# Opening of a spectral-filter-plus-MLP kernel: transposes paired by part, part of the first transform done early, another order for the weights

## The chip, the cores and the metric

The kernel runs on one core of a Trainium2 chip. A core has five engines with an instruction queue each: TensorE (PE in the profile, its weight loads PEld), VectorE (DVE), ScalarE (ACT), GpSimd (POOL) and SyncE (SP), which here only issues DMAs. The time is device microseconds (us) of one launch. Three runs of the kernel before took 394.82, 395.14 and 395.75 us; the median, 395.14 us, is the time that the prediction is set against.

## The reference, cut to what matters

```python
def reference(A_x, A_w_r, A_w_i, B_x, B_w1, B_b1, B_w2):
    x = A_x                                   # 1 x 2048 x 512, float32
    xn = (x - mean) / sqrt(var + 1e-5)        # over the last axis
    X = rfft2(xn) * (A_w_r + 1j * A_w_i)      # spectral filter over both axes
    h = einsum("bsd,df->bsf", xn, B_w1) + B_b1        # 512 -> 1792
    act = h * tanh(softplus(h))                       # Mish
    return x + irfft2(X, s=(2048, 512)) + einsum("bsf,fd->bsd", act, B_w2)
```

Every matrix product is made from float16 parts: a float32 operand is split into a high part and a low part (what the high part leaves over), and three products (high by high, high by low, low by high) are summed in PSUM. To fit float16's range a weight matrix is scaled by a power of two that is taken from a norm of it.

## The kernel before, in words

**Tiling.** The 2048 rows are four groups g of four row tiles of 128. The MLP is worked as 56 up tiles (g, f): hidden chunk f (14 chunks of 128) for the 512 rows of group g, twelve matmuls of 512 columns (three products for each of four blocks dc of the input, `mlp_up`, L744), and 56 down tiles (`mlp_down`, L800) that add a chunk's part of the output into four PSUM banks `pa`, twelve matmuls again. For group 0 and even f the down tile takes its four matmuls with the low part of w2 last (L806). A call b(1) runs one up or one down tile, whichever `mlp_all` (L837) picks: the first E_UP = 11 are up tiles, then ups and downs by a lag and by free buffers for the activations `a`. An up tile's sum `ph` lives in a pool of two PSUM banks (`ps_h`, L53), which the transposes of row tiles (`pt`) also use. `activate` (L761) follows an up tile: Mish on ACT (`hb`, L767), the high part of `a` on ACT (L785), its low part on DVE (L788).

**Opening** (`first_group`, L226). Rows of group 0 are normalised: the high part of a row tile on ACT (L239), its float32 value on DVE (`normed`, L249) and from that the low part on DVE (`low`, L254). PE transposes each part in four 128-column pieces (`turn_`). One PSUM bank `pt[s]` holds the high and low part of one row tile s; DVE copies the high half out and ACT the low half (`copy`, L261) into `xnT`, the moving operand of the up tiles. Matmuls on a tile of zeros (`idle_matmuls`, L221) fill PE between them. Meanwhile ACT squares w1's chunks 0 and 1 for their norm (L396), POOL sums over partitions (L326), DVE makes the scale (`w1_scale`, L411) and ACT and DVE split chunk 0 into high (`split_hi`) and low (`split_lo`). w1 comes in seven chunks of 256 hidden columns, c = f // 2; chunks 2 to 6 have a norm of their own (`w1_norm(1)`): two by squares on ACT, three by BN_STATS on DVE (L403). `act_scale` (L432) bounds the hidden values from these norms, for the scale of `a`. All of w2 must have a norm (`norm_w2`, L447) before its first split.

**The order** on ACT and DVE (in the opening also on PE) is the order in which the code is written (`in_order`, L67), so an instruction that waits holds all behind it on its engine.

**Slots** (L1023). After the opening, 26 slots of one b(1) each carry the rest of the preparation: statistics of the next group (`sums`, `factors`), normalising (`norm`, L202, with the low part on POOL), transposes (`turned_rows`, L297, copied out by DVE at L306), the first transform step of every row tile (`s1_forward`, L137, three matmuls into `psS`, from a pool of two banks `ps_f`; evicted by ACT and DVE at L123, L127, L128 in `butterfly`) and w2's chunks (high part on ACT, L468; low part on DVE one slot later, L471). In a slot come first the tile, then the last slot's leftovers (copies of `pt`, low parts of `a`, evictions of `psS`, low part of w2), then this slot's own work. The row tiles of group 0 have their transform step in slots 0 to 3.

**After the slots**, `stream_a` (L911) runs the middle transform steps with MLP tiles between them, and the end runs the last inverse step (`s1_inverse`) with the last tiles.

Of the kernel before, what the change touches and what calls it, by code (L numbers as in the profile page):

```python
# [41 lines left out]
def spectral_mlp_kernel(ctx, tc, x, wt, w0, w1, b1, w2, cT, cIT, cM, out):  # L42
# [183 lines left out]
    def first_group(ts):  # L226

        pe, act, dve = mybir.EngineType.PE, mybir.EngineType.Activation, mybir.EngineType.DVE
        with in_order(pe, act, dve):
            idle_matmuls(29)  # L230
            mv, rs, nb = factors(0, sums(0, ts, range(4)))
            xh, xs, pt = {}, {}, {}
            xnT[0] = cp.tile([P, 2, 4, 512], F16, tag="xnT0", name="xnT_0")
            xTv = xnT[0].rearrange("p h c (s t) -> p h c s t", s=4)

            def high(s):

# [14 lines left out]

            def low(s):
                nc.vector.tensor_sub(xh[s][:, 1, :], xs[s], xh[s][:, 0, :])  # L254

            def turn_(s, h):
                if not h:
                    pt[s] = ps_h.tile([P, 2, 4, P], F16, tag="h", name=f"pt_{s}")
                turn(pt[s], xh[s], h)

            def copy(s):  # L261
                nc.vector.tensor_copy(xTv[:, 0, :, s, :], pt[s][:, 0])
                return nc.scalar.copy(xTv[:, 1, :, s, :], pt[s][:, 1])


            qs = w1_norm(0, lambda: high(0))
            for s in range(1, 4):
                high(s)
            normed(0)
            normed(1)  # L270
            low(0)
            turn_(0, 0)
            turn_(1, 0)
            turn_(0, 1)
            low(1)
            turn_(1, 1)
            idle_matmuls(6)
            copy(0)
            w1_scale(0, qs)
            normed(2)  # L280
            normed(3)
            split_hi(0)
            low(2)
            turn_(2, 0)
            idle_matmuls(4)
            turn_(2, 1)
            copy(1)
            low(3)
            turn_(3, 0)
            idle_matmuls(2)  # L290
            turn_(3, 1)
            idle_matmuls(2)
            copy(2)
            ends = [copy(3).ins, split_lo(0).ins]
        return [xh[s] for s in range(4)], ends

    def turned_rows(g, s, xh):  # L297
        if s == 0:
# [88 lines left out]
    def w1_norm(k, between=None):  # L387

        a, b = W1_PARTS[k]
        n = min(b - a, 3)  # L390
        q = sp.tile([P, n], F32, tag=f"qw{k}", name=f"qw1_{k}")
        for c in range(a, a + 2):
            if between and c > a:
                between()
            fs = slice(2 * c * P, (2 * c + 2) * P)
            nc.scalar.activation(w1t[:, 0, :, fs], w1st[c], AF.Square, accum_out=q[:, c - a : c - a + 1])  # L396
        if b - a > 2:
            m = b - a - 2
            st = sp.tile([P, 2 * m, 6], F32, tag="stw", name="stw")
            for c in range(a + 2, b):  # L400
                v = w1st[c].rearrange("p c f -> p (c f)")
                for h in range(2):
                    nc.vector.bn_stats(st[:, 2 * (c - a) - 4 + h, :], v[:, 512 * h : 512 * h + 512])  # L403
            mv = sp.tile([P, 2], F32, tag="mvw", name="mvw")
            nc.vector.bn_aggr(mv, st)
            t = q[:, 2:3]
            nc.vector.scalar_tensor_tensor(t, mv[:, 0:1], mv[:, 0:1], mv[:, 1:2], op0=ALU.mult, op1=ALU.add)
            nc.vector.tensor_scalar(t, t, 1024.0 * m, None, op0=ALU.mult)
        return sum_of(f"w1_{k}", q, n)

    def w1_scale(k, t):  # L411
        p1 = pow2_norm(f"w1_{k}", t, min(W1_PARTS[k][1] - W1_PARTS[k][0], 3))
# [19 lines left out]
    def act_scale():  # L432
# [4 lines left out]
        nc.vector.scalar_tensor_tensor(hb_, pmx, 46.0, sc["mba"], op0=ALU.mult, op1=ALU.add)  # L437
        pH = pow2_of("H", hb_)
        sc["a"] = over("a", pH, 14)
        sc["pH"] = pH  # L440
# [297 lines left out]


    macc, yacc, last, wait, in_a = {}, {}, {}, [], []  # L740
    sc["ahead"], sc["staged"] = True, False
    staged, lows = [], []

    def mlp_up(g, f, acts):  # L744
# [1 line left out]
        ph = ps_h.tile([P, 512], F32, tag="h", name=f"ph_{g}_{f}")  # L746

        steps = [(dc, p) for dc in range(4) for p in range(3)]
        if g == f == 0:
            steps = [(dc, p) for p in range(3) for dc in range(4)]  # L750
        for n, (dc, p) in enumerate(steps):
            hs, hm = ((0, 0), (0, 1), (1, 0))[p]
# [8 lines left out]
    def activate(g, f, acts, ph, last_mm):  # L761
# [16 lines left out]
        wait.append((a, hb))  # L778
        if g == 0 and f < 2:
            return  # L780
        if g == 0 and f in (2, 3):
            split_w1(f)
        while wait:
            a, hb = wait.pop(0)
            hi = nc.scalar.activation(a[:, 0, :], hb, AF.Copy, scale=sc["a"])  # L785
# [51 lines left out]
    def mlp_all():  # L837
# [4 lines left out]
        while down < len(tiles):  # L842
# [4 lines left out]
            if free and up < len(tiles) and (up < E_UP or up - down < lag or (n_down >= 2 and up - down > lag)):  # L847
# [95 lines left out]
    load_w1(1)  # L943
    nc.sync.dma_start(cMt[:, O_ID:], cM[:, O_ID:])
    nc.sync.dma_start(b1t, b1)
    for c in range(2, 7):
        load_w1(c)
    load_ct(0)
    for c in range(7):
        load_w2(c)  # L950
    xs = {1: load_x(1)}
    xhs, ends = first_group(xs0)
    with tc.issue_after(ends[0]), tc.issue_after(ends[1]), in_order(mybir.EngineType.Activation, mybir.EngineType.DVE):

# [43 lines left out]
    for g, (a, ns, ts) in {  # L998
# [19 lines left out]
    copies, evict, low_w2 = [], [], []  # L1018
# [242 lines left out]
```

## Time and profile before

| quantity | value |
|---|---|
| median of three runs | 395.14 us (394.82 to 395.75) |
| the profiled execution | 394.64 us, of which its span (first to last instruction) 392.9 us |
| PE busy | 379.6 us, 97% of the span |
| DVE, ACT, POOL busy | 248.3, 203.8, 59.8 us (63%, 52%, 15%) |
| DMA | 61.61 MB, mean 157 GB/s |
| granted TensorE clock, mean over the span | 0.998 of full speed |

Times in the views are us from the span's start. A row of the timeline merges like instructions that follow each other on an engine: start, length, engine, line, operation, output and inputs, shapes, count, and in brackets the engine's idle time before it with what ended that. Matmuls are pipelined: a row of n matmuls is as long as n steps from start to start plus the rest of the last one, which is longer than a step. So time lost by PE is read from starts, not from the bracket alone.

### The profile page before, as it was taken

Reading aid. Unit: us, or ns where it says so; the run is one execution under the profiler, and the core shown is the slowest. Engines: PE = TensorE matmul, PEld = TensorE weight load, DVE = VectorE, ACT = ScalarE, POOL = GpSimd, SP = SyncE. Lnnn points to the kernel's source line nnn. Section 1 sums busy time; section 2 is a strip of 40 time slices with the busy share of each in tenths; the row PEclk is TensorE's granted clock in tenths of the full one; section 3 lists DMA queues with packets and bytes.
Section 4 is the critical chain, followed back from the end, with each engine's and each line's share of the span. In section 5 each row is a group of like instructions: output and inputs, shape, how many; then the busy total and the mean of one; then the engine's idle time right before and its main releaser. Section 6 shows DMA issues by size and latency. Waiting matters only on the chain. (4 is left out here: it accounts for less than half of the span.)

```text
span 392.9 us, 6538 instructions
## 1 busy us (share of the span) xinstructions
PE 379.6 (97%) x2481; PEld 190.7 (49%) x2481; DVE 248.3 (63%) x532; ACT 203.8 (52%) x325; POOL 59.8 (15%) x61
## 2 busy tenths in 40 slices
PE   8799999999999999999999999999999999999995
PEld 3344444545545454456444565455554546434442
DVE  5789793868578426974797535965449863324334
ACT  3869849677544336563554636365464455422110
POOL 0000015644523300000111100121001110210000
PEclk9999999999999999999999999999999999999999
DMA  8996021555347982066722727227561023654556
GB/s 280 364 395 276 1 82 45 171 178 163 103 133 231 249 236 81 24 147 159 237 82 62 201 64 211 83 81 197 180 188 55 27 82 91 205 160 138 165 194 253
DMA packets 49519, 61.61 MB, mean 157 GB/s; under 512 B 3776, under 2 KB 36032, under 8 KB 48848
## 3 DMA queue, kind: packets, MB, share of 16 engines
q1 hardware_dynamic: 49488, 61.20, 50.5%
q8 instruction: 19, 0.31, 0.3%
q14 instruction: 12, 0.10, 0.1%
HBM read 44.38 MB, written 16.78 MB: 156 GB/s over the span
## 5 line engine op out<-in xcount | busy, mean ns | idle before, releaser
L753 PE MATMUL ph<-xnT,w1t 128*128 128x512 f16 x672 | 153.5, 379 | 1.0 <-DVE w1t L352 0.5
L753 PEld LDWEIGHTS <-w1t 128*128 128x128 f16 x672 | 64.7, 98 | 78.2 <-DVE w1t L352 1.0
L88 PE MATMUL pa<-w2r,a 128*128 128x512 f16 x196 | 74.4, 380 | 0.0
L91 PE MATMUL pa<-w2r,a 128*128 128x512 f16 x196 | 74.4, 379 | 0.0
L92 PE MATMUL pa<-w2r,a 128*128 128x512 f16 x196 | 74.3, 379 | 0.0
L788 DVE SCALAR_TENSOR_TENSOR a<-hb,sc_a,a 128x512 f16<-128x512 f32 x56 | 42.2, 757 | 50.1 <-ACT a L785 49.8
L767 ACT ACTIVATE hb<-ph,b1t,sc_exp 128x512 f32<-128x512 f32 x56 | 43.2, 771 | 57.6 <-PE ph L753 57.5
L133 POOL TENSOR_TENSOR tt<-bt_t,tt 128x512 f16<-128x512 f32 x16 | 19.8, 1240 | 184.2 <-ACT tt L132 177.9
L785 ACT ACTIVATE a<-hb,sc_a 128x512 f16<-128x512 f32 x56 | 40.1, 720 | 1.5
L92 PEld LDWEIGHTS <-a 128*128 128x128 f16 x196 | 19.2, 98 | 22.5
L88 PEld LDWEIGHTS <-a 128*128 128x128 f16 x196 | 19.1, 98 | 21.9 <-issue 0.8
L91 PEld LDWEIGHTS <-a 128*128 128x128 f16 x196 | 19.2, 98 | 21.2 <-issue 0.8
L351 ACT ACTIVATE u<-r,sc_u 128x512 f16<-128x512 f32 x16 | 11.5, 720 | 23.9 <-DVE r L651 16.4
L133 POOL TENSOR_TENSOR y<-bt_s,y 128x512 f16<-128x512 f32 x16 | 19.1, 1194 | 31.4 <-ACT y L132 28.7
L132 ACT CAST y<-bt_s 128x512 f16<-128x512 f32 x16 | 9.9, 617 | 21.1 <-DVE bt_s L128 17.3
L808 PE MATMUL pa<-w2r,a 128*128 128x512 f16 x84 | 19.4, 379 | 0.6 <-DVE w2r L471 0.3
L132 ACT CAST tt<-bt_t 128x512 f16<-128x512 f32 x16 | 9.9, 616 | 15.9 <-DVE bt_t L128 13.5
L887 DVE SCALAR_TENSOR_TENSOR m<-psY,sc_k,m 128x512 f32<-128x512 f32 x12 | 8.7, 747 | 14.9 <-PE psY L92 14.9
L210 POOL TENSOR_TENSOR xh<-xs,xh 128x512 f16<-128x512 f32 x12 | 15.6, 1305 | 15.8 <-ACT xh L209 14.4
L706 DVE SCALAR_TENSOR_TENSOR at<-psA,at 128x512 f16<-128x512 f32 x16 | 10.7, 688 | 8.8 <-ACT at L705 8.8
L583 ACT ACTIVATE ix<-psD 64x512 f32<-64x512 f32 x16 | 9.5, 594 | 10.9 <-PE psD L571 10.7
L705 ACT ACTIVATE at<-psA 128x512 f16<-128x512 f32 x16 | 9.1, 590 | 10.5 <-issue 5.9
(146 smaller groups left out, 519.5 us busy)
## 6 DMA issues: line engine op xcount, KB each, us to landing
wt<-in_wt_dram SPq DMA_DIRECT2D x32, 256.0 KB
x<-in_x_dram SPq DMA_DIRECT2D x8, 512.0 KB
d_y<-y SPq DMA_DIRECT2D x16, 256.0 KB
wm<-in_wt_dram SPq DMA_DIRECT2D x8, 512.0 KB
yt<-d_y SPq DMA_DIRECT2D x16, 256.0 KB
d_a<-at SPq DMA_DIRECT2D x32, 128.0 KB
ai<-d_a SPq DMA_DIRECT2D x16, 256.0 KB
d_t<-tt SPq DMA_DIRECT2D x16, 256.0 KB
```

The source lines that it names most:

```text
L88: first = nc.tensor.matmul(ps, stat(0), mov(0), start=start, stop=False)
L91: nc.tensor.matmul(ps, stat(0), mov(1), start=False, stop=False)
L92: return nc.tensor.matmul(ps, stat(1), mov(0), start=False, stop=stop)
L132: nc.scalar.copy(out[:, :, 0, :], tv)
L133: nc.gpsimd.tensor_sub(out[:, :, 1, :], tv, out[:, :, 0, :])
L210: nc.gpsimd.tensor_sub(xh[:, 1, :], xs, xh[:, 0, :])
L351: hi = nc.scalar.activation(dst_h, src, AF.Copy, scale=scale)
L753: last_mm = nc.tensor.matmul(ph, w1t[:, hs, dc, f * P : (f + 1) * P], xnT[g][:, hm, dc, :], start=n == 0, stop=n == 11)
L767: nc.scalar.activation(hb, ph, AF.Mish, bias=b1t[:, f : f + 1], scale=s_exp[k])
L785: hi = nc.scalar.activation(a[:, 0, :], hb, AF.Copy, scale=sc["a"])
L788: lo = nc.vector.scalar_tensor_tensor(a[:, 1, :], hb, sc["a"], a[:, 0, :], op0=ALU.mult, op1=ALU.subtract)
L808: nc.tensor.matmul(pacc[g][s], a[:, ha, rows[s]], w2t[:, f // 2, hw, 0, :], start=f == n == 0, stop=False)
```

## The change

- The two row tiles 2k and 2k+1 share PSUM banks by part: `pt[k, 0]` holds both high parts, `pt[k, 1]` both low parts. One DVE copy (`copy_hi`) and one ACT copy (`copy_lo`) of 1024 columns stand for two each of 512.
- High parts of row tiles 0 and 1 are both made on ACT ahead of the square of w1's chunk 1. The order of the other steps changes, and 8 idle matmuls stand where 14 stood.
- The first transform step of row tiles 2 and 3 runs in the opening, beside their last transposes; its evictions run in slot 0. Its constants (`load_ct(0)`) are loaded ahead of w1's chunks 2 to 6 instead of after them. Row tiles 0 and 1 follow in slots 1 and 2.
- For three chunks of w1 the norm takes maxima (TENSOR_REDUCE) instead of BN_STATS, and `act_scale` has 92 for 46.
- Twelve up tiles come first instead of eleven. Splits of w1 and norms of w2 stand in another order among them; the splits of chunk 1 and 3 no longer hang on `activate`.
- For group 0 every even up tile takes its products part by part (four matmuls of each), so the low part of its w1 chunk is needed at the ninth matmul instead of the third; before, tile 0 alone did.
- No up tile of a group starts before the copies of that group's four row tiles are in the program (`sc["rows"]`); with this, tile 14 (group 1, chunk 0) comes later among the down tiles.

```diff
-E_UP = 11
+E_UP = 12
@@ first_group
             def turn_(s, h):
-                if not h:
-                    pt[s] = ps_h.tile([P, 2, 4, P], F16, tag="h", name=f"pt_{s}")
-                turn(pt[s], xh[s], h)
-
-            def copy(s):
-                nc.vector.tensor_copy(xTv[:, 0, :, s, :], pt[s][:, 0])
-                return nc.scalar.copy(xTv[:, 1, :, s, :], pt[s][:, 1])
+                if s % 2 == 0:
+                    pt[s // 2, h] = ps_h.tile([P, 4, 2, P], F16, tag="h", name=f"pt_{s}_{h}")
+                for dc in range(4):
+                    nc.tensor.transpose(pt[s // 2, h][:, dc, s % 2, :], xh[s][:, h, dc * P : (dc + 1) * P], ident)
+
+            def copy_hi(k):
+                nc.vector.tensor_copy(xTv[:, 0, :, 2 * k : 2 * k + 2, :], pt[k, 0])
+
+            def copy_lo(k):
+                return nc.scalar.copy(xTv[:, 1, :, 2 * k : 2 * k + 2, :], pt[k, 1])

-            qs = w1_norm(0, lambda: high(0))
-            for s in range(1, 4):
-                high(s)
+            qs = w1_norm(0, lambda: (high(0), high(1)))
+            high(2)
+            high(3)
             normed(0)
             normed(1)
             low(0)
+            low(1)
             turn_(0, 0)
             turn_(1, 0)
             turn_(0, 1)
-            low(1)
             turn_(1, 1)
-            idle_matmuls(6)
-            copy(0)
-            w1_scale(0, qs)
+            idle_matmuls(3)
+            copy_hi(0)
             normed(2)
             normed(3)
-            split_hi(0)
+            copy_lo(0)
             low(2)
             turn_(2, 0)
+            idle_matmuls(1)
+            turn_(3, 0)
+            w1_scale(0, qs)
+            split_hi(0)
             idle_matmuls(4)
+            low(3)
+            copy_hi(1)
             turn_(2, 1)
-            copy(1)
-            low(3)
-            turn_(3, 0)
-            idle_matmuls(2)
+            evict = [s1_forward(0, 2, xh[2])]
             turn_(3, 1)
-            idle_matmuls(2)
-            copy(2)
-            ends = [copy(3).ins, split_lo(0).ins]
+            evict.append(s1_forward(0, 3, xh[3]))
+            ends = [copy_lo(1).ins, split_lo(0).ins]
@@ w1_norm
-            for c in range(a + 2, b):
-                v = w1st[c].rearrange("p c f -> p (c f)")
-                for h in range(2):
-                    nc.vector.bn_stats(st[:, 2 * (c - a) - 4 + h, :], v[:, 512 * h : 512 * h + 512])
-            nc.vector.bn_aggr(mv, st)
...
+        for c in range(a + 2, b):
+            nc.vector.tensor_reduce(q[:, c - a : c - a + 1], w1st[c], axis=AX.XY, op=ALU.max, apply_absolute_value=True)
         if b - a > 2:
+            nc.vector.tensor_mul(q[:, 2:n], q[:, 2:n], q[:, 2:n])
@@ mlp_up, activate, mlp_all
-        if g == f == 0:
+        if g == 0 and f % 2 == 0:
             steps = [(dc, p) for p in range(3) for dc in range(4)]
...
-        if g == 0 and f in (2, 3):
-            split_w1(f)
...
+            free = free and up < len(tiles) and tiles[up][0] <= sc["rows"]
@@ the loads and the opening's tiles
+    load_ct(0)
     for c in range(2, 7):
         load_w1(c)
-    load_ct(0)
...
         bias_max()
+        qs = w1_norm(1)
         split_w1(1)
-        w1_scale(1, w1_norm(1))
+        b(2)
+        w1_scale(1, qs)
+        split_hi(2)
         act_scale()
-        b(4)
+        split_lo(2)
+        b(2)
+        split_w1(3)
         norm_w2(3)
+        b(1)
         norm_w2(4)
         b(1)
         split_w1(4)
+        norm_w2(0)
+        b(1)
         norm_w2(5)
+        norm_w2(1)
         b(1)
-        norm_w2(0)
+        split_w1(5)
         norm_w2(6)
         b(1)
-        split_w1(5)
-        b(1)
-        norm_w2(1)
         norm_w2(2)
         b(1)
@@ the slots
-    for s in range(4):
-        at[s]["turn"].append((0, s))
+    for s in range(2):
+        at[s + 1]["turn"].append((0, s))
```

What stands on ACT in the opening before, from the first copy of a low part (`pt`, into `xnT`) on; `w1s_k` is w1's chunk k, L420 and L351 are high parts, L396 squares, `hb_0_f` the Mish of up tile f:

```order
L263 COPY xnT_0_187<-pt_0_206 128x4x128
L420 ACTIVATE w1t_92<-w1s_0_100,sc_w1_0_240 128x4x256
L263 COPY xnT_0_187<-pt_1_211 128x4x128
L263 COPY xnT_0_187<-pt_2_250 128x4x128
L263 COPY xnT_0_187<-pt_3_267 128x4x128
L351 ACTIVATE w1t_92<-w1s_1_102,sc_w1_0_240 128x4x256
L396 ACTIVATE w1t_92,qw1_1_293<-w1s_2_106 128x4x256 x2
L767 ACTIVATE hb_0_0_342<-ph_0_0_329,b1t_94,sc_exp_0_242 128x512
L767 ACTIVATE hb_0_1_358<-ph_0_1_345,b1t_94,sc_exp_0_242 128x512
L767 ACTIVATE hb_0_2_374<-ph_0_2_361,b1t_94,sc_exp_0_242 128x512
L351 ACTIVATE w1t_92<-w1s_2_106,sc_w1_1_315 128x4x256
```

And the same place on ACT now:

```order
L267 COPY xnT_0_187<-pt_0_1_216 128x4x256
L420 ACTIVATE w1t_92<-w1s_0_100,sc_w1_0_253 128x4x256
L267 COPY xnT_0_187<-pt_2_1_265 128x4x256
L403 ACTIVATE w1t_92,qw1_1_288<-w1s_2_107 128x4x256 x2
L358 ACTIVATE w1t_92<-w1s_1_102,sc_w1_0_253 128x4x256
L768 ACTIVATE hb_0_0_312<-ph_0_0_299,b1t_94,sc_exp_0_255 128x512
L768 ACTIVATE hb_0_1_328<-ph_0_1_315,b1t_94,sc_exp_0_255 128x512
L420 ACTIVATE w1t_92<-w1s_2_107,sc_w1_1_337 128x4x256
L768 ACTIVATE hb_0_2_366<-ph_0_2_353,b1t_94,sc_exp_0_255 128x512
```

Four copies became two of twice the size, and the high part of chunk 2 moved ahead of the Mish of tile 2.

On DVE in slots 4 to 7 before stand the evictions of the first transform step (`bt_s1_s`, row tile s), the low parts of w2 (L471, here chunks 2 and 3), the copy of row tile 4's transpose (L306) and the low part of up tile 12's `a`:

```order
L127 SCALAR_TENSOR_TENSOR bt_s1_2_685<-psS1_2_662,bc_s1_2_683 128x4x64
L128 SCALAR_TENSOR_TENSOR bt_s1_2_685<-psS1_2_662,bc_s1_2_683 128x4x64
L471 SCALAR_TENSOR_TENSOR w2r_93<-w2r_93,sc_w2_515 128x1024
L127 SCALAR_TENSOR_TENSOR bt_s1_3_716<-psS1_3_697,bc_s1_3_714 128x4x64
L128 SCALAR_TENSOR_TENSOR bt_s1_3_716<-psS1_3_697,bc_s1_3_714 128x4x64
L471 SCALAR_TENSOR_TENSOR w2r_93<-w2r_93,sc_w2_515 128x1024
L306 COPY xnT_1_764<-pt_4_765 128x8x128
L788 SCALAR_TENSOR_TENSOR a_0_12_780<-hb_0_12_778,sc_a_327,a_0_12_780 128x512
L127 SCALAR_TENSOR_TENSOR bt_s1_4_799<-psS1_4_774,bc_s1_4_797 128x4x64
```

And on DVE now, around the same two low parts of w2:

```order
L787 SCALAR_TENSOR_TENSOR a_0_12_680<-hb_0_12_678,sc_a_350,a_0_12_680 128x512
L127 SCALAR_TENSOR_TENSOR bt_s1_1_698<-psS1_1_674,bc_s1_1_696 128x4x64
L128 SCALAR_TENSOR_TENSOR bt_s1_1_698<-psS1_1_674,bc_s1_1_696 128x4x64
L471 SCALAR_TENSOR_TENSOR w2r_93<-w2r_93,sc_w2_522 128x1024
L787 SCALAR_TENSOR_TENSOR a_0_13_750<-hb_0_13_748,sc_a_350,a_0_13_750 128x512
L471 SCALAR_TENSOR_TENSOR w2r_93<-w2r_93,sc_w2_522 128x1024
L311 COPY xnT_1_771<-pt_4_772 128x8x128
L127 SCALAR_TENSOR_TENSOR bt_s1_4_801<-psS1_4_781,bc_s1_4_799 128x4x64
```

The low part of up tile 13 now stands ahead of w2's chunk 3 and of the first copy of group 1; before it stood far behind both. On PE the tiles in slots 0 to 12 were down 0, 1, up 11, down 2, 3, 4, up 12, down 5, up 13, down 6, 7, 8, up 14; they are now down 0, 1, up 12, down 2, 3, up 13, down 4, 5, 6, 7, 8, up 14, down 9.

## Rows read from the trace of the kernel before

**Rows 1.** The page: span, busy time of the engines, GB/s in 40 slices.

```profile
span 392.9 us, 6538 instructions
...
PE 379.6 (97%) x2481; PEld 190.7 (49%) x2481; DVE 248.3 (63%) x532; ACT 203.8 (52%) x325; POOL 59.8 (15%) x61
...
GB/s 280 364 395 276 1 82 45 171 178 163 103 133 231 249 236 81 24 147 159 237 82 62 201 64 211 83 81 197 180 188 55 27 82 91 205 160 138 165 194 253
```

**Rows 2.** Waits of PE: line, waited for, us in total, times, longest.

```profile
PE psT L88 <- DMA ai<-d_a: 1.8, 3, 0.9
```

**Rows 3.** Timeline of PE, opening and slots.

```profile
1.17 8.46 PE L224 MATMUL ps_warm<-warm 128*128 128x512 f16 x29 [1.17 <-DVE warm L219]
...
11.73 1.12 PE L215 MATMUL pt<-cMt,xh 128*128 128x128 f16 x12 [1.34 <-ACT xh L239]
...
17.77 10.96 PE L753 MATMUL ph<-xnT,w1t 128*128 128x512 f16 x50
29.22 17.87 PE L753 MATMUL ph<-xnT,w1t 128*128 128x512 f16 x82 [0.48 <-DVE w1t L352]
47.38 2.75 PE L808 MATMUL pa<-w2r,a 128*128 128x512 f16 x12 [0.29 <-ACT w2r L351]
...
62.92 1.89 PE L808 MATMUL pa<-w2r,a 128*128 128x512 f16 x8
65.11 1.02 PE L808 MATMUL pa<-w2r,a 128*128 128x512 f16 x4 [0.30 <-DVE w2r L471]
...
83.30 2.75 PE L808 MATMUL pa<-w2r,a 128*128 128x512 f16 x12
...
113.72 2.76 PE L753 MATMUL ph<-xnT,w1t 128*128 128x512 f16 x12 [0.38 <-DVE xnT L306]
```

**Rows 4.** Timeline of ACT, opening and slots.

```profile
10.88 2.21 ACT L239 ACTIVATE xh<-x,nb,rs 128x512 f16<-128x512 f32 x3
...
13.73 1.15 ACT L420 ACTIVATE w1t<-w1s,sc_w 128x1024 f16<-128x1024 f32 x1 [0.17 <-DVE sc_w L345]
...
46.18 1.15 ACT L351 ACTIVATE w2r<-w2r,sc_w 128x1024 f16<-128x1024 f32 x1 [1.64 <-DVE sc_w L345]
...
59.33 0.62 ACT L132 CAST y<-bt_s 128x512 f16<-128x512 f32 x1 [4.35 <-DVE bt_s L128]
...
60.91 0.76 ACT L767 ACTIVATE hb<-ph,b1t,sc_exp 128x512 f32<-128x512 f32 x1
61.70 0.72 ACT L785 ACTIVATE a<-hb,sc_a 128x512 f16<-128x512 f32 x1
...
62.59 0.80 ACT L206 ACTIVATE xs<-x,nb,rs 128x512 f32<-128x512 f32 x1
```

**Rows 5.** Timeline of DVE, opening and slots.

```profile
9.97 0.69 DVE L254 TENSOR_TENSOR xh<-xs,xh 128x512 f16<-128x512 f32 x1
...
12.73 0.14 DVE L333 TENSOR_REDUCE qt_w<-qs_w 128x1 f32<-128x2 f32 x1
...
14.52 0.69 DVE L254 TENSOR_TENSOR xh<-xs,xh 128x512 f16<-128x512 f32 x1
...
20.61 3.65 DVE L403 BATCH_NORM_STATS2 stw<-w1s 128x6 f32<-128x512 f32 x6
...
33.28 1.21 DVE L453 TENSOR_REDUCE q<-w2r 128x1 f32<-128x1024 f32 x1
...
44.57 0.75 DVE L788 SCALAR_TENSOR_TENSOR a<-hb,sc_a,a 128x512 f16<-128x512 f32 x1 [0.87 <-ACT a L785]
...
71.95 1.24 DVE L788 SCALAR_TENSOR_TENSOR a<-hb,sc_a,a 128x512 f16<-128x512 f32 x1 [0.84 <-ACT a L785]
...
82.09 1.28 DVE L471 SCALAR_TENSOR_TENSOR w2r<-w2r,sc_w 128x1024 f16<-128x1024 f32 x1
```

**Rows 6.** Line L306, DVE's copies: duration ns, minimum/median/maximum.

```profile
L306 DVE COPY xnT<-pt x12: 658/682/693, 70.4 to 123.7; 128x1024 f16<-128x1024 f16 x12
```

**Rows 7.** Timeline of POOL: the low part of one row tile.

```profile
64.12 1.96 POOL L210 TENSOR_TENSOR xh<-xs,xh 128x512 f16<-128x512 f32 x1 [2.94 <-ACT xh L209]
```

More of the change, by code (lines that the diff above doesn't have):

```diff
@@ L274, in first_group @@
             turn_(0, 1)
-            low(1)
             turn_(1, 1)
-            idle_matmuls(6)
-            copy(0)
-            w1_scale(0, qs)
+            idle_matmuls(3)
+            copy_hi(0)
             normed(2)
             normed(3)
-            split_hi(0)
+            copy_lo(0)
             low(2)
             turn_(2, 0)
+            idle_matmuls(1)
+            turn_(3, 0)
+            w1_scale(0, qs)
+            split_hi(0)
             idle_matmuls(4)
+            low(3)
+            copy_hi(1)
             turn_(2, 1)
-            copy(1)
-            low(3)
-            turn_(3, 0)
-            idle_matmuls(2)
+            evict = [s1_forward(0, 2, xh[2])]
             turn_(3, 1)
-            idle_matmuls(2)
-            copy(2)
-            ends = [copy(3).ins, split_lo(0).ins]
-        return [xh[s] for s in range(4)], ends
+            evict.append(s1_forward(0, 3, xh[3]))
+            ends = [copy_lo(1).ins, split_lo(0).ins]
+        return [xh[s] for s in range(4)], ends, evict
     def turned_rows(g, s, xh):
@@ L306, in copies @@
             nc.vector.tensor_copy(xTv[:, :, :, s, :], pt)
+            if s == 3:
+                sc["rows"] = g
         return copies
@@ L389, in w1_norm @@
         a, b = W1_PARTS[k]
-        n = min(b - a, 3)
+        n = b - a
         q = sp.tile([P, n], F32, tag=f"qw{k}", name=f"qw1_{k}")
@@ L396, in w1_norm @@
             nc.scalar.activation(w1t[:, 0, :, fs], w1st[c], AF.Square, accum_out=q[:, c - a : c - a + 1])
+        for c in range(a + 2, b):
+            nc.vector.tensor_reduce(q[:, c - a : c - a + 1], w1st[c], axis=AX.XY, op=ALU.max, apply_absolute_value=True)
         if b - a > 2:
-            m = b - a - 2
-            st = sp.tile([P, 2 * m, 6], F32, tag="stw", name="stw")
-            for c in range(a + 2, b):
-                v = w1st[c].rearrange("p c f -> p (c f)")
-                for h in range(2):
-                    nc.vector.bn_stats(st[:, 2 * (c - a) - 4 + h, :], v[:, 512 * h : 512 * h + 512])
-            mv = sp.tile([P, 2], F32, tag="mvw", name="mvw")
-            nc.vector.bn_aggr(mv, st)
-            t = q[:, 2:3]
-            nc.vector.scalar_tensor_tensor(t, mv[:, 0:1], mv[:, 0:1], mv[:, 1:2], op0=ALU.mult, op1=ALU.add)
-            nc.vector.tensor_scalar(t, t, 1024.0 * m, None, op0=ALU.mult)
+            nc.vector.tensor_mul(q[:, 2:n], q[:, 2:n], q[:, 2:n])
         return sum_of(f"w1_{k}", q, n)
     def w1_scale(k, t):
-        p1 = pow2_norm(f"w1_{k}", t, min(W1_PARTS[k][1] - W1_PARTS[k][0], 3))
+        p1 = pow2_norm(f"w1_{k}", t, W1_PARTS[k][1] - W1_PARTS[k][0])
         w1sc[k] = over(f"w1_{k}", p1, 14)
@@ L436, in act_scale @@
         hb_ = sp.tile([P, 1], F32, tag="hb_", name="hb_")
-        nc.vector.scalar_tensor_tensor(hb_, pmx, 46.0, sc["mba"], op0=ALU.mult, op1=ALU.add)
+        nc.vector.scalar_tensor_tensor(hb_, pmx, 92.0, sc["mba"], op0=ALU.mult, op1=ALU.add)
         pH = pow2_of("H", hb_)
@@ L740, in spectral_mlp_kernel @@
     macc, yacc, last, wait, in_a = {}, {}, {}, [], []
-    sc["ahead"], sc["staged"] = True, False
+    sc["ahead"], sc["staged"], sc["rows"] = True, False, 0
     staged, lows = [], []
@@ L846, in mlp_all @@
             free = down >= up - up % 4 - 8 if home else len(in_a) < NA or in_a[-NA] < down
-            if free and up < len(tiles) and (up < E_UP or up - down < lag or (n_down >= 2 and up - down > lag)):
+            free = free and up < len(tiles) and tiles[up][0] <= sc["rows"]
+            if free and (up < E_UP or up - down < lag or (n_down >= 2 and up - down > lag)):
                 mlp_up(*tiles[up], acts)
@@ L951, in spectral_mlp_kernel @@
     xs = {1: load_x(1)}
-    xhs, ends = first_group(xs0)
+    xhs, ends, evict = first_group(xs0)
     with tc.issue_after(ends[0]), tc.issue_after(ends[1]), in_order(mybir.EngineType.Activation, mybir.EngineType.DVE):
         bias_max()
+        qs = w1_norm(1)
         split_w1(1)
-        w1_scale(1, w1_norm(1))
+        b(2)
+        w1_scale(1, qs)
+        split_hi(2)
         act_scale()
-        b(4)
+        split_lo(2)
+        b(2)
+        split_w1(3)
         norm_w2(3)
+        b(1)
         norm_w2(4)
@@ L1017, in spectral_mlp_kernel @@
     sc["staged"] = True
-    copies, evict, low_w2 = [], [], []
+    copies, low_w2 = [], []
     _, hi, lo = last["up"]
```

## The prediction

> **What bounds the kernel now.** The page first: PE is busy 97% of the span of 392.9 us, every other engine at most 63% [rows 1]. So time can only come from stretches in which PE runs no useful matmul, and the timeline of PE shows where those are. One is the opening: 29 matmuls on zeros, then transposes between which PE waits, and the first up tile starts at 17.77 [rows 3]. The others are stalls. A step from one 512-column matmul to the next is 0.216 us: 82 of them take 17.87, the last one counted in full [rows 3]. From 17.77, 50 steps end at 28.57, and the next matmul starts at 29.22: 0.65 lost to the low part of w1's chunk 2. From 29.22, 82 steps end at 46.93, and the first down tile starts at 47.38: 0.45 lost to the high part of w2. From 62.92, 8 steps end at 64.65, resumed at 65.11: 0.46 to a low part of w2. At 113.72 an up tile waits for a copy, 0.38 by its bracket [rows 3]. Behind that the largest waits are for a DMA in the inverse steps (psT, 1.8 in three) [rows 2]. Last I read ACT and DVE around these places [rows 4, 5].
>
> **The change part by part.**
>
> *The start of the first up tile.* In the old order DVE's low part of row tile 1 waited for ACT, which squared a w1 chunk first; PE's twelve transposes started at 11.73 after 1.34 idle [rows 3]. Now ACT makes that high part directly behind the first. The first is there when DVE starts low(0) at 9.97 [rows 5], a high part steps by some 0.72 (three in 2.21 [rows 4]), so the second is there near 10.7 and DVE starts low(1), right behind low(0) (9.97 and 0.69). From then DVE runs without a wait: low(1) 0.69, copy_hi 0.68 (the same 1024 columns take 0.68 in the slots [rows 6]), both normed tiles with the scale chain 1.79 (12.73 to 14.52 [rows 5]), low(2) and low(3) 0.69 each. That is 10.7 + 4.5 = 15.2; copy_hi(1) ends at 15.9. ACT's split_hi(0) starts when the scale is there, about 14.5, takes 1.15 [rows 4] and ends at 15.65; copy_lo(1) follows, bounded by half and double of split_hi's 1.15 for the same 1024 columns; I take 1.0. PE does row tile 2's transform step (3 x 0.216) while it waits for low(3), then the last transposes (four, 0.2) and row tile 3's step: 15.2 + 0.2 + 0.65 = 16.1. So the first up tile starts between 16.1 and 16.6, with copy_lo(1) due only at its fifth matmul. With the parts in banks of their own an ACT copy waits for PE alone; late next is low(3).
>
> *Up to the first down tile.* Before, 132 up matmuls were done at 47.38. Now 144 and the six of the transform steps must be, and 144 x 0.216 = 31.1 gives 47.2 to 47.7 if nothing waits. Does anything? The norm of w1's rest no longer stalls: three maxima of 1.21 [rows 5] replace six statistics of 3.65 in all [rows 5], which is the same, and one multiplication stands for three small steps. But they start at about 17 instead of 20.61, behind copy_hi(1) and split_lo(0), so chunk 2's parts come some 3.6 sooner; tile 4 comes 1.4 sooner and lost 0.65 before, which leaves 1.5 of slack, and it now asks for the low part at its ninth matmul. I cost the maxima at nothing; that slack is their cover. The transform constants ahead of w1 cost 0.26 MB at 364 GB/s [rows 1], 0.7 us on chunks 2 to 6; by the same rates 5.0 MB are in at about 16, before DVE reads at 17. ACT sets the other end. Before, w2's first high part started at 46.18, 1.61 after a low part of a had started on DVE (44.57 [rows 4, 5]). Now one tile's Mish and high part of a, 0.76 and 0.72 [rows 4], come ahead of it as well, and the tiles come 1.4 to 2.0 sooner: 45.7 to 46.3, and with its 1.15 it is there at 46.8 to 47.4. PE needs it at 47.2 at the earliest. I take 47.4. Before, the same 150 matmuls were done at 47.38 + 18 x 0.216 = 51.27. **The opening gives 3.9**: 1.4 from the start, 1.3 from six matmuls in idle places, 1.1 from two stalls.
>
> *The slots.* Here the sum goes back. DVE and ACT did not get the same lead. All of ACT's next work starts behind y of row tile 0, which waits for DVE as y of row tile 1 did before (59.33, after 4.35 idle [rows 4]); two more evictions stand ahead of it, so I put it at 60.2. Then ACT is busy without a gap to the high part of a of tile 13: y to xs is 3.26 (59.33 to 62.59), three times xs and xh 0.80 and 0.62, a y 0.62, a high part of w2 1.15, Mish and a 1.48 [rows 4]: 10.8 by lengths, of which neighbours overlap a little at their ends; 10.5, so 70.7. DVE's low part of tile 13 waits for it, and queued behind it are now w2's chunk 3, the copies of group 1 and all that leads to the low part of w2's chunk 4. Before, that run took 10.14 from the low part of tile 12 (71.95 to 82.09 [rows 5]). Now tile 13's low part is out of its middle (0.66), the low part of chunk 3 (1.2) and one copy (0.6) are in it, and 0.5 of slack at its head is not: 10.8. Chunk 4's low part starts at 81.5 and ends, after 1.28, at 82.8. Down tile 8 asks for it at its ninth matmul: before at 83.30 + 1.73 = 85.03, 1.66 after it was there (82.09 + 1.28 [rows 3, 5]). Now PE would be 3.9 ahead, and another 0.3 since the stall at 65.11 shrinks to some 0.2: 80.7. **PE waits 2.1 there**, and leads by 2.2 behind it. Tile 14's own copies are done 0.7 after chunk 4's low part, so holding it costs nothing beside this.
>
> *Behind it.* Before, DVE had slack in the next slots, and up tile 17 waited at 113.72; now its bank is free earlier in the order: +0.4. The middle steps keep their work but stand between other MLP tiles. The psT wait (1.8 in all [rows 2]) may grow or go with two to four matmuls more or less in front of each wait, up to 0.9 either way; some transform steps are cut once more by MLP matmuls. I take 0, with 1.0 on both sides.
>
> *Sum.* 3.9 + 0.3 - 2.1 + 0.4 + 0 = 2.5. The profiled execution took 394.64, of which 392.9 is span and 1.7 lies around it, unchanged: 392.1. It stands 0.5 under the median of 395.14; against the median the forecast is **392.6**.
>
> *A rule that speaks against it.* TENSOR_REDUCE on 1024 columns took 1.21 and two statistics of 512 took 1.22 (3.65 / 6 x 2) [rows 5]. The Trainium skill's page "VectorE: DVE Perf Modes" (section "The perf-mode tier table") lists tensor_reduce with the 1x mode alone and elsewhere calls it the slowest VectorE operation. By that the maxima would be a loss; by the rows they are none, and the sum is the same.
>
> **The rivals.**
>
> *The lead is kept.* DVE could finish chunk 4's low part earlier than I chain it: if ACT gets through its run with 2 us less, for example because y of row tile 0 does not wait behind the statistics of group 1. For it: ACT sat idle 4.35 there before. Against it: the order is fixed. Then the gain is 3.9 + 0.3 + 0.4 = 4.6: 390.5.
>
> *The middle steps give more back.* PE reaches the first inverse step with four matmuls fewer behind its forward step, and psT's DMA chain does not shorten: 0.9 more, and the two more cuts cost 0.2 to 0.4. Gain 1.2: 393.9.
>
> *Slower: POOL holds ScalarE's run.* ACT's xs has two buffers, each free only when POOL's low part is done. One such low part took 1.96 [rows 7]. If the four of group 1 take that, each queued behind a y, ACT's run stretches by up to 2 x 2 and tile 13's low part comes at 74.5; chunk 4's low part then ends 4 later, down tile 8 and each copy behind wait for it. PE loses 6.1 instead of 2.1: 396.6 by that, and slower than before once the stretch passes 2.5. Against it: POOL is busy 59.8 of 392.9 [rows 1], and the lows ran while ACT had other work.
>
> *The clock falls in the opening.* The first 29 matmuls took 8.46 [rows 3], against 29 x 0.216 = 6.3: 2.1 is what a start at the lower level (1.2 GHz instead of 2.4) cost. With 8 idle matmuls instead of 14 PE could fall back and pay that again: 394.7. Against it: PE idled 1.34 at 11.73 and the following steps still ran at 0.216; the new gaps are shorter. The Trainium skill's page "TensorE: Matmul & The Clock Gate" (Part 1) says that "the default state is throttled, and activity releases the throttle"; by it fewer idle matmuls are a risk, and the rows so far show none.
>
> **How the numbers follow.** The forecast 0.53, the kept lead 0.20, the middle steps 0.15, POOL 0.07, the clock 0.05. A measurement of this kernel tells 0.2%, 0.8 us, from no change: faster is below 394.35, slower above 395.9. The forecast's own range is 391.2 to 394.0 (1.0 on the middle steps, 1.0 on the chain to chunk 4). To leave out no more than 2 in 10 it reaches to the kept lead below and to the clock above: 390.4 to 394.7. Faster: nearly all of the first two and two thirds of the third, 0.82; same 0.12; slower 0.06.
>
> **What would show it.** First up tile near 16.3; no wait of an up tile before the first down tile, which starts near 47.4; ACT's Mish of tile 13 at about 69; the largest wait of PE in the slots in down tile 8, on DVE's low part of w2, 1.5 to 2.5. Wrong it is if PE passes down tile 8 without a wait (then the kept lead), or if an earlier tile waits for w1 or w2 by over 0.5 us (then the opening was over-counted).

## The result, and the profile after

The changed kernel is slower: 396.28 us, median of nine runs (395.98 to 397.83), against 394.82 (394.16 to 395.75) for the kernel before on the same chip. The ratio of all runs is 1.0049 with an interval of 1.0031 to 1.0068; by the medians alone it is 1.0037, because four of the nine times lie apart at 397.50 and above. The forecast was 392.6, and the range up to 394.7 does not hold the measured time. The profiled execution took 395.98, with a span of 394.2 that stands against 392.9 in [rows 1]. The page after, its span and the busy time of the engines:

```profile
span 394.2 us, 6527 instructions
...
PE 378.9 (96%) x2475; PEld 190.6 (48%) x2475; DVE 248.4 (63%) x525; ACT 204.0 (52%) x323; POOL 60.3 (15%) x61
```

No engine has noticeably more work than before. PE has six matmuls fewer, the idle ones. So the 1.3 us are waits. Where they are shows first in PE's timeline, opening and slots (start, length, instructions, count, and in brackets the idle time before with what ended it), to be held against [rows 3]:

```profile
15.90 31.24 PE L754 MATMUL ph<-xnT,w1t 128*128 128x512 f16 x144
47.61 2.75 PE L807 MATMUL pa<-w2r,a 128*128 128x512 f16 x12 [0.46 <-ACT w2r L358]
...
64.61 1.89 PE L807 MATMUL pa<-w2r,a 128*128 128x512 f16 x8
66.86 1.02 PE L807 MATMUL pa<-w2r,a 128*128 128x512 f16 x4 [0.37 <-DVE w2r L471]
...
79.87 1.89 PE L807 MATMUL pa<-w2r,a 128*128 128x512 f16 x8
83.94 1.02 PE L807 MATMUL pa<-w2r,a 128*128 128x512 f16 x4 [2.18 <-DVE w2r L471]
84.80 2.75 PE L754 MATMUL ph<-xnT,w1t 128*128 128x512 f16 x12
```

The opening runs as forecast: 144 up matmuls without a wait from 15.90, and the first down tile at 47.61. Down tile 8 starts at 79.87, 3.43 ahead of [rows 3] (83.30), and waits in its middle: eight steps of 0.216 end at 81.60, the ninth starts at 83.94, 2.34 lost. Behind it up tile 14 starts at 84.80. In both kernels the same tiles and transform steps stand ahead of that start, so it is a mark by which leads are read below. The kernel before has it here:

```profile
85.89 2.75 PE L753 MATMUL ph<-xnT,w1t 128*128 128x512 f16 x12
```

So 1.09 of the lead is left at the mark. At the end of the span it is −1.3. The rest of the program, in which the diff changes only the condition for an up tile (`sc["rows"]`), loses 2.4.

That part, from 140 to 360, shows in the view of waits (line, waited for, us in total, times, longest) of the kernel after:

```profile
PE psT L88 <- DMA ai<-d_a: 1.7, 3, 1.0
PE psD L571 <- DVE bt_t L128: 1.4, 2, 0.9
PE psP L547 <- DVE z L560: 1.1, 3, 0.4
PE psY L88 <- DMA yi<-d_t: 0.8, 1, 0.8
PE psA L88 <- DVE at L706: 0.3, 2, 0.2
```

In the kernel before the psT row of [rows 2] stands in that stretch, and with it only these:

```profile
PE psD L571 <- DVE bt_t L128: 0.8, 1, 0.8
PE psY L88 <- DMA yi<-d_t: 0.8, 1, 0.8
PE psA L88 <- DVE z L560: 0.4, 1, 0.4
PE psP L547 <- DVE z L560: 0.2, 1, 0.2
PE psD L571 <- DVE at L706: 0.2, 1, 0.2
```

Eight waits of 4.2 in all have become eleven of 5.3. A bracket is less than the time lost, as two rows of after show:

```profile
173.22 0.38 PE L91 MATMUL pa<-w2r,a 128*128 128x512 f16 x1
173.96 1.53 PE L547 MATMUL psP<-cMt,yt 128*64 128x128 f16 x48 [0.36 <-DVE z L560]
```

From start to start 0.74 pass instead of a step of 0.216: 0.52 are lost where the bracket has 0.36. Counted so, the pauses over 0.25 us from 145 on sum to 7.7 after and 5.7 before, which is 2.0 of the 2.4.

### The profile page after: what moved, and what is told of

Its sections match the earlier page's. It is cut to its first block, busy times and chain, and to the rows that moved or that the text cites. A ratio compares the mean times of both kernels' runs of the same rounds, so it can differ in the third digit from the quotient of the medians.

```text
span 394.2 us, 6527 instructions
## 1 busy us (share of the span) xinstructions
PE 378.9 (96%) x2475; PEld 190.6 (48%) x2475; DVE 248.4 (63%) x525; ACT 204.0 (52%) x323; POOL 60.3 (15%) x61
## 4 chain that ended last, share of the span: by engine, by line
PE 61%; DVE 18%; ACT 10%; issue 4%; DMA 4%; POOL 1%; SPq 0%; POOLq 0%; DVEq 0%; ACTq 0%
PE ph L754 23%; PE pa L92 7%; PE pa L88 7%; PE pa L91 7%; PE psD L571 3%; PE pa L807 2%; DVE m L832 2%; ACT hb L768 2%; ACT a L784 2%; DVE a L787 2%; PE psP L547 2%; DVE st L188 1%; PE pt L215 1%; DVE w2r L471 1%; DMA x<-in_x_dram 1%
## 5 line engine op out<-in xcount | busy, mean ns | idle before, releaser
L571 PE MATMUL psD<-z,cMt 64*128 64x256 f16 x192 | 13.8, 270 | 1.4 <-DVE bt_t L128 1.4
```

What stands on the lines that cost most here:

```text
L571: first = nc.tensor.matmul(ps[be][:, k], c_d[rows, k0 + k, e, hs, :], z[rows, hm, 2 * (k0 + k) + e].rearrange("p g q -> p (g q)"), start=e ...
```

## The experiments

Two theories stood against each other on the 2.4. **Theory 1, the places:** with twelve up tiles in the opening the stream of middle steps starts with 38 half tiles done, not 37. Its quota (`done - start < used * (B_END - start) / N_WGT`) is counted from there, so every MLP tile falls at another place between the transform steps, and PE meets more short waits. **Theory 2, the lead:** chains that end at a fixed time take back whatever PE is ahead.

After and the ten variants in one table: the ratio of all runs to those of the kernel before with its interval; then, from the profiled execution, the start of up tile 14, the lead there over 85.89, the lead at the end (392.9 less the span), and what the part between gave back.

| kernel | half tiles done | median us | ratio | up tile 14 | lead | lead at the end | given back |
|---|---|---|---|---|---|---|---|
| after | 38 | 396.28 | 1.0049 [1.0031, 1.0068] | 84.80 | 1.1 | −1.3 | 2.4 |
| e1: 25 slots | 37 | 396.10 | 1.0018 [1.0002, 1.0034] | 85.30 | 0.6 | −1.5 | (clock) |
| e2: before, 27 slots | 38 | 397.48 | 1.0076 [1.0054, 1.0097] | 86.08 | −0.2 | −2.7 | 2.5 |
| e3: sums early | 38 | 395.43 | 1.0010 [1.0002, 1.0019] | 83.99 | 1.9 | −0.5 | 2.4 |
| e4: both | 37 | 393.76 | 0.9963 [0.9951, 0.9975] | 84.10 | 1.8 | 0.9 | 0.9 |
| e5: factors late | 37 | 394.18 | 0.9975 [0.9964, 0.9985] | 84.55 | 1.3 | 0.8 | 0.5 |
| e6: and wt late | 37 | 392.97 | 0.9948 [0.9936, 0.9960] | 84.61 | 1.3 | 1.7 | −0.4 |
| e7: steps in slots | 38 | 394.85 | 0.9991 [0.9980, 1.0002] | 83.86 | 2.0 | −0.9 | 2.9 |
| e8: 24 slots | 36 | 393.72 | 0.9967 [0.9957, 0.9978] | 84.09 | 1.8 | 0.4 | 1.4 |
| e9: steps, 25 slots, wt | 37 | 392.15 | 0.9935 [0.9923, 0.9947] | 83.78 | 2.1 | 1.7 | 0.4 |
| e10: and sums early | 37 | 391.68 | 0.9918 [0.9905, 0.9932] | 83.34 | 2.6 | 3.4 | −0.8 |

A profiled execution lies up to 0.85 off its kernel's median (e9), so differences of less than a microsecond in the last column say little.

**e1, 25 slots.** One number in the kernel after. It also moves the ten steps that take maxima of the spectral weights (`N_SLOTS - 10` on) to one slot earlier:

```diff
-N_SLOTS = 26
+N_SLOTS = 25
```

> The kernel after with 25 slots instead of 26, and nothing else: the stream of middle steps then starts with 37 half tiles done, as in the kernel before, and places its MLP tiles between the transform steps nearly as that kernel did. Theory 1 (phase: the twelfth up tile in the opening shifts the count from which the stream deals out its tiles, and the new places make PE wait more): the loss of some 2.5 us behind 145 us goes, and the time is about 393.8. Theory 2 (the loss behind 145 us hangs on the lead itself: chains that end at a fixed time take back whatever PE gained): no change, about 396.3. Both expect the stall of 2.3 us in down tile 8 (at 81 us) to stay.

Inconclusive by itself: its twelve times reach from 394.13 to 397.66. The profile (of one of 396.24) shows one reason. Windows of PE behind the stall in down tile 8 (busy, instructions, granted clock, DMA share, GB/s):

```profile
82.00:84.00 2.00, 0.01 (x1) 1.00 0.00 0
84.00:86.00 2.00, 1.82 (x6) 0.69 0.00 0
86.00:88.00 2.00, 2.00 (x6) 0.50 0.44 131
```

PE stood still from 81.85 to 84.18; then the granted clock fell to 0.50, the 1.2 GHz level, and up tile 14 took 4.18 instead of 2.75. In the profiled execution of after the same wait left the clock at 1.00. Five runs of e1 lie between 394.13 and 395.04, 0.3 to 1.2 above what theory 1 expects, and none of after's is under 395.98; the variants with a shorter stall below tell it better.

**e2, the kernel before with 27 slots.** The counterpart, one number in the kernel before:

```diff
-N_SLOTS = 26
+N_SLOTS = 27
```

> The kernel before with 27 slots instead of 26, and nothing else: its opening and slots stay as they are, but the stream of middle steps starts with 38 half tiles done, as in the kernel after, and deals out its tiles nearly as that one does. Theory 1 (phase): slower than the kernel before by 2 to 2.6 us, about 397.2. Theory 2 (the lead): there is no lead here to give back, so about 394.9.

Slower by 2.2 by medians, 2.7 by span, and 2.5 of that behind the mark, which comes 0.2 later than in the kernel before:

```profile
86.08 2.75 PE L753 MATMUL ph<-xnT,w1t 128*128 128x512 f16 x12
```

The waits from 140 to 360:

```profile
PE psD L571 <- DVE bt_t L128: 1.5, 2, 1.0
PE psT L88 <- ACT tt L132: 1.1, 1, 1.1
PE psP L547 <- DVE z L560: 0.9, 3, 0.4
PE psY L88 <- DMA yi<-d_t: 0.8, 1, 0.8
PE psT L88 <- DMA ai<-d_a: 0.7, 2, 0.3
PE psA L88 <- DVE at L706: 0.3, 2, 0.2
```

Eleven waits of 5.3, at the same steps as in after: three at psP, two at psA, two at psD, three at psT. A kernel with no lead to give back loses the same 2.5. Theory 2 falls here. The moved maxima (here to one slot later) are not the cause either: after has them where the kernel before has them, and waits as e2 does.

**e3, the statistics of row group 2 earlier** (slots 4 and 5 instead of 7 and 8), in after:

```diff
-        2: (7, (10, 11, 12, 13), (12, 13, 15, 16)),
+        2: (4, (10, 11, 12, 13), (12, 13, 15, 16)),
```

> The kernel after with the statistics of row group 2 in slots 4 and 5 instead of 7 and 8, nothing else; the stream's order is that of the kernel after. If DVE's queue in slots 7 and 8 holds the low part of w2's chunk 4 back, the stall in down tile 8 shrinks from 2.3 to under 0.5 us, and the lead over the kernel before at 95 us is 3 to 3.5 instead of 1.1. If ScalarE's run (the high part of a of tile 13) holds it, the stall stays over 1.8. At the end: theory 1 (phase) keeps what is gained, about 394.2; theory 2 (the lead is given back in any case) 396.3.

The stall leaves down tile 8, but one of 1.35 turns up two tiles earlier, so 0.8 is won and not 2. It is in down tile 6, at the low part of w2's chunk 3; where the expectations below speak of down tile 7, this tile is meant. PE and VectorE there:

```profile
72.68 1.89 PE L807 MATMUL pa<-w2r,a 128*128 128x512 f16 x8
75.76 1.02 PE L807 MATMUL pa<-w2r,a 128*128 128x512 f16 x4 [1.19 <-DVE w2r L471]
```

```profile
66.91 1.28 DVE L188 BATCH_NORM_STATS2 st<-x 128x6 f32<-128x512 f32 x2
...
69.83 0.44 DVE L196 TENSOR_SCALAR ve<-mv 128x4 f32<-128x4 f32 x1
70.30 1.08 DVE L161 TENSOR_SCALAR rr<-ve 128x4 int32<-128x4 int32 x1
...
72.87 0.74 DVE L787 SCALAR_TENSOR_TENSOR a<-hb,sc_a,a 128x512 f16<-128x512 f32 x1
73.54 2.18 DVE L471 SCALAR_TENSOR_TENSOR w2r<-w2r,sc_w 128x1024 f16<-128x1024 f32 x1
```

In after VectorE stood idle there for 5.02:

```profile
71.83 0.75 DVE L787 SCALAR_TENSOR_TENSOR a<-hb,sc_a,a 128x512 f16<-128x512 f32 x1 [5.02 <-ACT a L784]
```

The statistics and their factors take 5.96 (66.91 to 72.87), not the 6.2 of a later expectation, and so they run over. But 1.2 of it is two small steps that are stretched (0.44 and 1.08 instead of 0.17 each), and the low part of w2 behind them takes 2.18 instead of 1.28; the last section says by what. Without the stretching they would have fitted, by an estimate from these rows (4.8 into 5.0). By its time alone, 395.43, e3 lies between the two theories. The part behind the mark decides: it gives back 2.4 again, no more for the larger lead, so what was won stays won.

**e4, both edits** in after:

```diff
-N_SLOTS = 26
+N_SLOTS = 25
...
-        2: (7, (10, 11, 12, 13), (12, 13, 15, 16)),
+        2: (4, (10, 11, 12, 13), (12, 13, 15, 16)),
```

> The kernel after with both edits: 25 slots, and the statistics of row group 2 in slots 4 and 5. Theory 1 (phase, and the two losses add): the stall of 2.3 and the 2.5 behind 145 us are both gone, about 391.5, faster than both kernels. Theory 2: 396.3; if the two are not independent, between 392.5 and 394.

Faster than both kernels, though 2.3 short of what theory 1 expected, and within the range named for two losses that are not independent. Against e3, which has the same work ahead of the mark and nearly the same lead there, 25 slots are worth 1.7 by medians. The expectation, written before e3 ran, did not have the stall's new place, nor one new wait in the middle, PE's timeline:

```profile
226.87 0.86 PE L547 MATMUL psP<-cMt,yt 128*64 128x128 f16 x24 [1.02 <-DMA yt<-d_y]
```

**e5, the factors of group 2 in slot 9** in e4's kernel, behind the low part of w2's chunk 4:

```diff
-        if 3 in ss:
+        if 3 in ss and g != 2:
             mr[g] = factors(g, mv[g])
+
+    def factors_2():
+        mr[2] = factors(2, mv[2])
...
+    at[9]["then"].append(factors_2)
```

> The kernel with both edits of before (25 slots, statistics of row group 2 in slots 4 and 5), and with the last step of those statistics, the factors of group 2 (3.1 us of small VectorE steps, which stood ahead of the low part of tile 13's a), moved to slot 9, behind the low part of w2's chunk 4. If VectorE's queue makes the remaining stall of 1.36 in down tile 7, it goes, down tile 8 still passes, and the lead over the kernel before at 95 us is about 3.2 instead of 1.8: about 392.5. If the low part waits for ScalarE or for GpSimd's share of the port, the stall stays at 1 or moves to down tile 8 with the same size: 393.8.

A miss. Down tiles 6 and 8 pass, but now the copies stand behind the factors, and up tile 14 waits for them:

```profile
84.55 2.75 PE L754 MATMUL ph<-xnT,w1t 128*128 128x512 f16 x12 [1.70 <-DVE xnT L311]
```

In these two kernels the other order only decides which tile waits for VectorE. By medians e5 is 0.4 slower than e4, which the two intervals do not keep apart.

**e6, and half of wt later.** In e5's kernel the be = 1 half of the next class's spectral weights is loaded behind that class's yt loads:

```diff
-            if c < 3:
+            if c < 3 and be == 0:
                 load_wt(c + 1, be)
...
+                    if c and g == 2:
+                        load_wt(c, 1)
```

> The kernel above, and half of the next class's spectral weights (1 MB of the 2 MB of wt) loaded behind the class's yt loads instead of ahead of them. The second psP unit at 225 us waited 1.0 for its yt load, issued among eight wt loads. If the wt loads' traffic makes that wait, it goes: 1.2 us faster than the kernel above, about 391.3. If the wait is for the stores of y or for something else in the queue, nothing changes; if the late half comes too late for the spectral products, PE waits at psA or psD instead, and it is slower than the kernel above by up to 2.

1.2 faster, as expected. No psP wait for yt is left. SyncE's queue shows what changed, e5 first and then e6:

```profile
220.17 0.33 SPq L734 DMA_DIRECT2D d_t<-tt  x1
220.55 0.47 SPq L526 DMA_DIRECT2D wt<-in_wt_dram  x1
221.11 0.54 SPq L536 DMA_DIRECT2D yt<-d_y  x1
```

```profile
216.09 0.33 SPq L536 DMA_DIRECT2D yt<-d_y  x1
```

The yt load is issued 5.0 sooner, ahead of a store (`d_t`) behind which it stood before. So its place in the queue has changed as well as the traffic beside it, and e6 does not tell the two apart. With the places of the kernel before and this wait gone, the middle gives nothing back (−0.4).

**e7, the two transform steps in the slots again**, the one part of the change undone:

```diff
-            evict = [s1_forward(0, 2, xh[2])]
-            evict.append(s1_forward(0, 3, xh[3]))
...
-    for s in range(2):
-        at[s + 1]["turn"].append((0, s))
+    for s in range(4):
+        at[s]["turn"].append((0, s))
```

> The kernel after with one part of the change undone: the first transform steps of row tiles 2 and 3 stand in slots 2 and 3 again (0 to 3 for all four), not in the opening. The stream's order is that of the kernel after. The opening then gains 1.3 less (2.6 instead of 3.9 at the first down tile's row of work). If the stall at down tile 8 is set by VectorE's and ScalarE's queues, which keep their time, it shrinks by about as much (from 2.3 to about 1.0), and the kernel takes the same time as after, 396.3 with 0.4 either way. If the stall is a fixed delay behind PE's own work, it stays at 2.3 and the time is 397.6.

Better than either theory: the stall in down tile 8 shrinks to 0.7, and the kernel is 1.4 faster than after by medians (its profiled execution, 395.54, is the longest of eleven). The lead at the mark is 2.0, not 1.1. ScalarE, VectorE and PE, one row of each:

```profile
59.63 0.62 ACT L132 CAST y<-bt_s 128x512 f16<-128x512 f32 x1 [4.35 <-DVE bt_s L128]
```

```profile
81.67 1.27 DVE L469 SCALAR_TENSOR_TENSOR w2r<-w2r,sc_w 128x1024 f16<-128x1024 f32 x1
```

```profile
83.00 1.02 PE L805 MATMUL pa<-w2r,a 128*128 128x512 f16 x4 [0.56 <-DVE w2r L469]
```

In after the first two rows stand at 61.08 and 82.61:

```profile
61.08 0.62 ACT L132 CAST y<-bt_s 128x512 f16<-128x512 f32 x1 [5.57 <-DVE bt_s L128]
```

```profile
82.61 1.27 DVE L471 SCALAR_TENSOR_TENSOR w2r<-w2r,sc_w 128x1024 f16<-128x1024 f32 x1
```

The steps that gave PE 1.3 in the opening put their evictions at the head of slot 0, and this y comes 1.45 later for it. Some 0.7 of that is the evictions' own time on VectorE (1.33 for four of them; 0.64 for the two of slot 1, which are gone from there). The rest stands in one row of after:

```profile
55.28 1.70 DVE L471 SCALAR_TENSOR_TENSOR w2r<-w2r,sc_w 128x1024 f16<-128x1024 f32 x1 [0.33 <-ACT w2r L468]
```

VectorE waits 0.33 for the high part of w2, ahead of which ScalarE now has two y, and the low part itself takes 1.70 where e7 has 1.27, beside two instructions of GpSimd (53.62 to 55.90). ScalarE's run behind the y holds one y and one eviction fewer in after, which makes good 0.5, and so chunk 4's low part comes 0.94 later. PE, whose time there is set by that chain, lost all of the 1.3 and 0.94 more.

**e8, 24 slots** in e3's kernel, 36 half tiles done:

```diff
-N_SLOTS = 26
+N_SLOTS = 24
```

> The kernel after with the statistics of row group 2 in slots 4 and 5 and 24 slots: the stream of middle steps starts with 36 half tiles done, one fewer than in the kernel before, and deals out its tiles in a third way. With 26 slots (38 done) this took 395.4, with 25 (37 done) 393.8. Theory 1a (each half tile done ahead of the stream leaves it one less to fill its waits with): at least as good as 25 slots, 393.0 to 393.8. Theory 1b (only where the tiles fall between the steps counts): not ordered by the count, anywhere from 393 to 396.5, and more likely slower than 25 slots, whose places the kernel before was fitted to.

As good as 25 (393.72 against 393.76), with 1.4 given back in the trace against 0.9, and its waits stand at other steps (psD for `at` 1.2, psY 0.9, a down tile for `m` 0.7). Its profiled execution, 394.28, is the longest of seven. It does not tell the two readings of theory 1 apart: whether one tile more to fill with helps, or only where the tiles fall, stays open.

**e9, three edits together**: in e7's kernel 25 slots and e6's loads.

```diff
-N_SLOTS = 26
+N_SLOTS = 25
...
+                    if c and g == 2:
+                        load_wt(c, 1)
```

> The kernel after with three edits: the transform steps of row tiles 2 and 3 in the slots again, 25 slots, and half of the next class's spectral weights loaded behind the yt loads. The statistics of row group 2 stay in slots 7 and 8. If the three losses are independent, the lead over the kernel before is 2.0 at 95 us (as with the steps in the slots alone), is kept through the middle steps (nearly the order of the kernel before, and no wait for yt) and ends at about 2.2: 392.5, some 2.7 under the kernel before. If the middle steps give back part of any lead, it ends where the kernel with both losses mended and a lead of 1.3 ended, at 393.0 or above.

392.15, somewhat better than expected by its median. Its profiled execution (393.0, the longest of five) keeps 2.1 until the first inverse step, where psT waits 1.5 for its DMA.

**e10, and e3's statistics** in e9's kernel:

```diff
-        2: (7, (10, 11, 12, 13), (12, 13, 15, 16)),
+        2: (4, (10, 11, 12, 13), (12, 13, 15, 16)),
```

> The kernel above with the statistics and factors of row group 2 in slots 4 and 5. In the kernel above some 0.7 is left of the stall in down tile 8. With the steps of row tiles 2 and 3 out of slot 0, VectorE waits 4.9 us for ScalarE ahead of the low part of tile 13's a, at 66 us; the statistics and factors take 6.2. If the excess of some 1.3 is all that reaches PE, the stall moves to down tile 7 with 0.5 to 1.0 us and the time is the same within 0.4. If GpSimd's low parts stretch VectorE's instructions there again (one took 2.18 instead of 1.28), the stall there is 1.4 and it is slower by 0.6.

The best kernel, 391.68, 0.8% under the kernel before, and better than expected. Small steps of VectorE are stretched again, but not the low part of w2's chunk 3: it ends at 75.06, against 75.72 in e3. So 0.40 is left of the stall in the slots, in down tile 6 (74.50 to 75.11, less a step), and the middle adds to the lead instead of taking from it.

## Why the prediction was wrong, point by point

The forecast gave a slower kernel a chance of 0.06.

*What held.* The opening's 3.9: 51.27 was the forecast's mark for the kernel before, and 47.61 makes it 3.7. The first up tile came at 15.90 (0.2 ahead of the range forecast), no up tile waited, the first down tile came at 47.61 (47.4). The largest wait stood where it was put, in down tile 8 on VectorE's low part of w2, 2.34 against 2.1. That the size fits so well is luck: PE asked at 81.60 instead of 80.7, and the low part ended at 83.88 instead of 82.8. The clock did not fall in the opening, and POOL held ScalarE's run by 0.18 (idle ahead of an xs at 67.86) and no more.

*The step that failed: "The middle steps keep their work but stand between other MLP tiles. ... I take 0, with 1.0 on both sides."* It cost 2.5, beyond that bound and beyond the 1.1 to 1.3 that the rival gave it: the forecast looked at psT alone, whose waits hardly changed, and the waits that came were at psP, psA and psD. That the shifted count does it is shown: in the kernel before the shift of the count by one costs 2.5 with no lead in play (e2); with the count as before e4 gives back 0.9 where e3 gives back 2.4, at the same lead; and with the yt loads freed as well, e6, e9 and e10 give back 0.4 at most, e10 from the largest lead of all. The prediction saw that the MLP tiles would fall elsewhere but priced it as neutral.

*A term mis-sized: "two more evictions stand ahead of it, so I put it at 60.2."* ScalarE's y came at 61.08. From there the chain ran as worked out within 0.2: chunk 4's low part started at 82.61 instead of 81.5, 1.1 late, and the lead behind down tile 8 was 1.1 and not 2.2. That the early transform steps are the cause is shown by e7, in which the y at the head of ScalarE's run comes at 59.63. The term had the evictions' own time; it had neither the wait for the high part of w2 nor the stretched low part. The rival that the lead is kept falls with it.

*Small ones.* The stall of down tile 4 did not shrink (0.52 lost, 0.2 forecast). The 0.4 at up tile 17 was won by less than half: from start to start PE lost 0.55 at that place and now loses 0.38. Two sums of the forecast are off by 0.1 to 0.2 and change nothing: 85.03 less 4.2 is 80.8, and 70.7 with 4 is 74.7.

The sum: 2.5 forecast less 1.1 (the chain), some 0.2 (up tile 17) and 2.5 (the middle) is −1.3, the difference of the spans. The rival "the middle steps give more back" had the right place and half the price.

*Not settled:* why the count of after costs PE this much and that of e8 less, and whether the places do it or the one tile fewer that is left to fill waits with. No rule for a good place was tried; the kernels only show that the places of the kernel before, and those of 24 slots, cost less.

## What to carry to other kernels

A change near the start can move a counter by which later work is dealt out; then the whole order behind it is new, and here that cost more (2.5) than was left of the early lead (1.1). Hold the counter (here the number of slots) while the early change is measured, and read the middle's waits as a list before and after. Early work on an engine that is ahead is no gain when its evictions land at the head of the queue on which that engine waits next.

## What the runs showed of the hardware that was not expected

*A small VectorE instruction can last as long as GpSimd's.* In e3 a step on 128 x 4 elements took 1.08 instead of 0.17 and ended at 71.38; these are POOL's rows beside it and beside the low part of w2:

```profile
69.09 2.27 POOL L210 TENSOR_TENSOR xh<-xs,xh 128x512 f16<-128x512 f32 x2
73.41 1.22 POOL L210 TENSOR_TENSOR xh<-xs,xh 128x512 f16<-128x512 f32 x1 [2.05 <-ACT xh L209]
```

The first ended at 71.36. The low part of w2 at 73.54 took 2.18 instead of 1.28 beside the second. Not every step is held: the statistics at 66.91 and 68.32 ran beside POOL's instructions too and kept their 1.28 and 1.25. The Trainium skill's page "Trainium Architecture — The Big Picture" (section "What this means for kernel authors") says that the port pair which VectorE and GpSimd share is an exclusive lock and no split of bandwidth; by that VectorE waits for the end of GpSimd's instruction, and the rows of the stretched steps agree.

*A wait of 2.2 us may or may not cost clock.* The same stall in down tile 8 left the granted clock at 1.00 in after's profile and brought it to 0.50 in e1's, where 1.7 more went: four matmuls took 1.12 from 84.18 to 85.30 instead of 0.86, and the up tile behind them 4.18 instead of 2.75. Where PE's longest stall in the slots was 1.4 or less (e3, e4, e7 to e10) a kernel's times lie within 1.1 us of each other; after's lie within 1.9 and e1's within 3.5. The clock need not be all of that: e2's times reach over 2.7 without such a stall, and those of the kernel before over 2.2.
